# Silu replaced by a tanh form in a fused attention and MLP kernel, and a new place for the output-weight conversions

## The chip, the cores and the metric

The kernel runs on one core of one Trainium2 chip. The metric is the device time of one execution in microseconds, and smaller is better. Before the change three runs took 964.84 to 966.88 us, with a median of 966.83 us.

## The reference

What is computed, cut to what matters here (batch 4, 8 heads, 576 positions, head size 64; 2304 tokens, model width 512, inner width 1536; all in float32):

```python
x = attention(q, k, v)             # heads 0-3: a local window of 32; heads 4-7: strided by 32
xn = x / rms(x) * rms_g
g = xn @ w_gate                    # 512 -> 1536
silu = g * (1.0 / (1.0 + np.exp(-g)))
y = (silu * (xn @ w_val)) @ w_out  # 1536 -> 512
out = ((y @ w_a) * (y @ w_b)) @ w_out2
```

## The kernel before

Matrix products are made in pairs of float32r words: each operand is split into a high part and a low part, and three products (high by high, high by low, low by high; lines 481 to 483) make one. The weights arrive from memory in 64-bit words. A conversion (`conversion`, `words`, `parts`) turns one third of a chunk's weights (gate, value or output) into these two parts: ScalarE runs a Prelu (L137) and a Copy into `cz` (L142), VectorE joins two words (L145), ScalarE casts the high part (L150), and GpSimd or VectorE subtracts it (L151). `cz` has two buffers for the gate and value weights and one for the output weights, so the conversions of the output weights run one behind the other.

The first half of the kernel handles the tokens in six blocks t = 0 to 5 of 384. Each block runs over 12 chunks fc of the inner width. For a chunk, TensorE makes `g_ps` and `v_ps` (12 matmuls each, in three PSUM banks with the tag `gv`). VectorE multiplies `g_ps` by the reciprocal norm `ri[t]` into `sg` (L774), ScalarE applies Silu in place (L776), and VectorE multiplies by `v_ps` into `h` (L787; in block 0 `h` is `v_ps` itself). `split` casts `h` to its high part on ScalarE (L506) and makes the low part on VectorE (block 0) or GpSimd (L507). One chunk later TensorE uses the two parts for the output products `y`. The temporaries `sg` and `h` share five buffers of the tag `t`.

Block 0 also converts the first layer's weights while it uses them: `convert1(fc + 1)` for gate and value, and the conversion of the output weights of chunk fc, which is stored to memory and reloaded in the later blocks. Beside the chunks of block t, the attention of block t+1 runs in steps: the local heads by TensorE with an Exp on ScalarE (L333, L336), the strided heads by GpSimd products (L248, L281) and VectorE reductions (L251, L284), an Exp (L264), then the norm with a Sqrt (L448). Block 5 has no next attention; it starts to convert the second layer's weights instead. The second half (from about 541 us) runs the second layer and has no Silu.

The order of instructions on each engine is fixed when the program is built, by a scheduler that works through the traced instructions with a modelled time. `behind(...)` and `gate(...)` bind it: they put every instruction of their block that runs on the engine of the named instruction behind that one. Two such bindings matter here. `exps` puts the local Exps of block 1's attention behind the newest Silu, and the next Silu behind them (`silu_gate`). The conversion of the output weights of chunks 2 to 11 stands behind the very first Silu, `silu[:1]`, on ScalarE's queue.

Of the kernel before, what the change touches and what calls it, by code (L numbers as in the profile page):

```python
# [14 lines left out]
AF = mybir.ActivationFunctionType  # L15
ALU = mybir.AluOpType
# [7 lines left out]
NTB = B * PB  # L24
# [53 lines left out]
def fused_kernel(ctx: ExitStack, tc: tile.TileContext, qtl, ktl, vl, qs, ks, vs, cst, w1, w2, out):  # L78
# [5 lines left out]
    nc = tc.nc  # L84
# [100 lines left out]
    ri = {}  # L185
# [304 lines left out]
    def tmp(name):  # L490
        return act.tile([128, NTB], F32, tag="t", name=name, bufs=NTMP)

    made = []
    silu, silu_gate = [], []

    @contextmanager
    def behind(instructions):

        with ExitStack() as e:
            for i in instructions:  # L500
                e.enter_context(tc.issue_after(i))
            yield
# [37 lines left out]
    def load_late(which):  # L540
        raw.update(zip(which, load_pair(w1, which, pool)))
# [39 lines left out]
    @contextmanager  # L581
    def gate(fc):

        with behind(silu[:1] if fc > 4 else []), ExitStack() as e:
            for key in GATES[min(fc, len(GATES) - 1)].split():
                e.enter_context(tc.issue_after(s0["st"][key].ins))
            yield
# [25 lines left out]
    def load_wo(t, fc):  # L613
        wt = wo[t, fc] = wo_tile()
        nc.sync.dma_start(wt.rearrange("p a n -> p (a n)").bitcast(F32), wod[fc])
# [14 lines left out]
        for n in part:  # L630
            steps[n]()

    def exps(steps):

        def together(f, key):
            def g():
                with behind([silu[-1]]):
                    f()
                silu_gate.append(steps["st"][key].ins)
            return g  # L640

        for n in ("lexp0", "lexp1", "lexp2"):
            steps[n] = together(steps[n], "exp")


    forms = {}

    def form_tile(k, spare=False):
# [93 lines left out]
    for t in range(NB):  # L742
        if t == 1:
            apool.close()
            pool = apool.enter_context(tc.tile_pool(name="attn", bufs=1))
        if t == NB - 1:
            apool.close()
            cpool.close()
            pool = p2.enter_context(tc.tile_pool(name="forms", bufs=1, reuse_waits="tile"))
            early = [f for k in (4, 5, 0, 1, 2, 3) for f in convert_forms(k, k < 4)]  # L750
        nxt = attention(t + 1, pool, psum, itertools.cycle(["att"])) if t + 1 < NB else None
        if t == 0:
            exps(nxt)
        x = [xt[t, cc] for cc in range(NCC)]
        for fc in range(NFC):
            if t > 0 and fc == 0:
                load_wo(t, 0)
            g_ps = psum.tile([128, 512], F32, tag="gv", name="g_ps", bufs=3)
            mm_in(g_ps[:, :NTB], gv[fc], 0, x)
            v_ps = psum.tile([128, 512], F32, tag="gv", name="v_ps", bufs=3)  # L760
            mm_in(v_ps[:, :NTB], gv[fc], 1, x)
            if t == 0 and fc + 1 < NFC:
                with gate(fc + 1):
                    convert1(fc + 1)
                if fc + 2 == NFC:
                    load_late([(NFC - 2, 2), (NFC - 1, 2)])
            if t == NB - 1:
                slab[fc] = wgt.tile([128, 4 * DM], F32 if fc in (0, 1, 11) else F32R, tag="gv", name="slab", bufs=NFC)
                with behind(made):
                    run(early[len(early) * fc // NFC:len(early) * (fc + 1) // NFC])  # L770
                    for k in [k for k in x0 if k <= fc]:
                        run(x0.pop(k))
            sg = tmp("sg")
            nc.vector.tensor_tensor(sg, g_ps[:, :NTB], ri[t], op=ALU.mult)  # L774
            with behind(silu_gate):
                silu.append(nc.scalar.activation(sg, sg, AF.Silu).ins)  # L776
            silu_gate[:] = []
            if fc == 1 and t > 0:
                evac_y(t - 1)
            if nxt is not None:  # L780
                attention_slot(nxt, fc)
            if prev is not None:
                emit_y(*prev)
            if t > 0 and fc + 1 < NFC:
                load_wo(t, fc + 1)
            h = tmp("h") if t else v_ps[:, :NTB]
            made[:] = [nc.vector.tensor_tensor(h, sg, v_ps[:, :NTB], op=ALU.mult).ins]  # L787
            hl[t, fc] = split(h, engine(HLO0[fc] if t == 0 else HLO[t]))
            if t == 0:
                wt = wo[0, fc] = wo_tile()  # L790
                with gate(fc + 1), behind(silu[:1] if fc > 1 else []):
                    run(conversion(raw.pop((fc, 2)), wt, pool, engine(WLO[fc][2]), LOW[fc][2], True))
                nc.sync.dma_start(wod[fc], wt.rearrange("p a n -> p (a n)").bitcast(F32))
                if fc % 2 and units:
                    load_units(1)
            prev = (t, fc)
# [140 lines left out]
    steps = [(ps, g, p) for ps in (range(0, 3), range(3, 6)) for g in range(NB // 2) for p in ps]  # L937
# [99 lines left out]
```

## Time and profile before

| | before |
|---|---|
| median of 3 runs | 966.83 us (964.84 to 966.88) |
| the profiled execution: its time / its span | 967.4 us / 965.6 us |
| TensorE matmuls busy | 937.1 us, 97% |
| VectorE busy | 621.5 us, 64% |
| ScalarE busy | 425.3 us, 44% |
| GpSimd busy | 539.5 us, 56% |
| mean granted TensorE clock | 0.985 |

The span runs from the first to the last instruction of the program; the time also holds what lies around it (1.8 us here). A busy TensorE works through pipelined matmuls; its idle time and the stretches at a lower granted clock are what another order of work can give back.

### The profile page before, as it was taken

To read this page: it belongs to the slowest core of one execution; us is meant where nothing else is said; L and a number is where in the kernel's file an instruction comes from. 1 tells how busy PE (TensorE), PEld (TensorE's weight loads), DVE (VectorE), ACT (ScalarE), POOL (GpSimd) and SP (SyncE) were. 2 spreads that over 40 slices of the span, in tenths; PEclk is the share of its full clock that TensorE was granted. 3 is DMA by queue.
4 is the path that set the end of the run, shared out by engine and by line. 5 is a ranking of instruction groups with operands and counts; after the bars stand their busy time and mean duration, and the time that the engine had idled before them with its cause. 6 is when DMAs were issued, how large, how long until landed. Compare 5 with 4: busy or idle time off the path is not lost.

```text
span 965.6 us, 14099 instructions
## 1 busy us (share of the span) xinstructions
PE 937.1 (97%) x5318; PEld 888.2 (92%) x5318; DVE 621.5 (64%) x900; ACT 425.3 (44%) x795; POOL 539.5 (56%) x407
## 2 busy tenths in 40 slices
PE   5998999999999999999999899999999999999998
PEld 4898999999999999999999898899999998999996
DVE  5658858658819895986666378658655655564534
ACT  5988646344433434434555455436425422122110
POOL 3567946558649677878479545655724423123211
PEclk6899999999999999999999999999999999999999
DMA  9974286537535563532788884996993974754701
GB/s 342 408 262 151 89 288 218 151 96 225 165 104 161 161 204 102 185 105 87 284 324 306 329 306 166 402 415 247 385 373 114 345 274 165 284 205 168 267 2 66
DMA packets 57363, 215.55 MB, mean 223 GB/s; under 512 B 5968, under 2 KB 14544, under 8 KB 51664
## 3 DMA queue, kind: packets, MB, share of 16 engines
q1 hardware_dynamic: 57296, 214.66, 61.3%
q8 instruction: 42, 0.69, 0.3%
q14 instruction: 25, 0.20, 0.1%
HBM read 172.17 MB, written 42.47 MB: 222 GB/s over the span
## 4 chain that ended last, share of the span: by engine, by line
PE 65%; DMA 11%; DVE 7%; POOL 7%; ACT 4%; issue 4%; SPq 0%; DVEq 0%; ACTq 0%; POOLq 0%
PE o L916 5%; PE o L918 5%; PE o L917 5%; DMA raw<-in_w 4%; POOL prod L248 4%; PE Y L862 4%; PE Y L861 4%; PE Y L860 4%; DMA gv_raw<-in_w 3%; PE y L482 3%; PE y L481 3%; PE g_ps L483 3%; PE y L483 3%; PE g_ps L482 3%; PE g_ps L481 3%
## 5 line engine op out<-in xcount | busy, mean ns | idle before, releaser
L151 POOL TENSOR_TENSOR hl<-c,hl 128x384 fp32r<-128x384 f32 x72 | 77.9, 1082 | 181.0 <-ACT hl L150 174.4
L248 POOL TENSOR_TENSOR prod<-kv_t,qs_t 128x512 f32<-128x512 f32 (+12 forms) x57 | 108.3, 1921 | 15.3 <-DMA kv_t<-in_ks 8.2
L481 PE MATMUL v_ps<-xx,gv 128*128 128x384 f32 x288 | 97.7, 339 | 1.9 <-DVE sg L774 1.8
L482 PE MATMUL y<-hl,wo 128*128 128x384 f32 x288 | 98.1, 341 | 1.1 <-POOL hl L507 1.1
L281 POOL TENSOR_TENSOR prod<-kv_t,S_t 128x512 f32<-128x512 f32 (+12 forms) x57 | 86.2, 1526 | 21.1 <-issue 7.1
L482 PE MATMUL v_ps<-xx,gv 128*128 128x384 f32 x288 | 97.9, 340 | 0.0
L483 PE MATMUL v_ps<-xx,gv 128*128 128x384 f32 x288 | 97.8, 340 | 0.0
L481 PE MATMUL g_ps<-xx,gv 128*128 128x384 f32 x288 | 97.5, 339 | 0.0
L483 PE MATMUL g_ps<-xx,gv 128*128 128x384 f32 x288 | 97.3, 338 | 0.0
L482 PE MATMUL g_ps<-xx,gv 128*128 128x384 f32 x288 | 96.9, 337 | 0.0
L867 DVE TENSOR_TENSOR c<-c,Y 128x384 f32<-128x384 f32 x108 | 59.0, 551 | 58.8 <-PE Y L862 53.5
L507 POOL TENSOR_TENSOR hl<-h,hl 128x384 fp32r<-128x384 f32 x60 | 64.1, 1069 | 58.4 <-ACT hl L506 57.3
L483 PE MATMUL y<-hl,wo 128*128 128x384 f32 x288 | 95.0, 338 | 0.0
L284 DVE TENSOR_REDUCE xs_t<-prod 128x64 f32<-128x448 f32 (+17 forms) x57 | 85.7, 1521 | 9.7 <-POOL prod L281 9.5
L481 PE MATMUL y<-hl,wo 128*128 128x384 f32 x288 | 85.0, 343 | 7.0 <-ACT hl L506 5.4
L916 PE MATMUL o<-slab,hl 128*128 128x512 f32 x216 | 84.7, 393 | 1.8 <-DVE slab L925 1.3
L917 PE MATMUL o<-slab,hl 128*128 128x512 f32 x216 | 84.5, 392 | 0.0
L918 PE MATMUL o<-slab,hl 128*128 128x512 f32 x216 | 83.2, 394 | 0.0
L150 ACT CAST hl<-c 128x384 fp32r<-128x384 f32 x72 | 37.0, 514 | 93.8 <-DVE c L897 93.5
L776 ACT ACTIVATE sg<-sg 128x384 f32<-128x384 f32 x72 | 38.0, 528 | 86.4 <-DVE sg L774 86.0
L862 PE MATMUL Y<-slab,form 128*128 128x384 f32 x216 | 73.0, 338 | 0.0
L861 PE MATMUL Y<-slab,form 128*128 128x384 f32 x216 | 73.0, 338 | 0.0
(137 smaller groups left out, 2491.4 us busy)
## 6 DMA issues: line engine op xcount, KB each, us to landing
form<-formd SPq DMA_DIRECT2D x32, 1792.0 KB, 10.7
wo<-wod SPq DMA_DIRECT2D x60, 512.0 KB, 3.8
raw<-in_w SPq DMA_DIRECT2D x40, 512.0 KB, 7.3
gv_raw<-in_w SPq DMA_DIRECT2D x32, 512.0 KB, 10.2
formd<-form SPq DMA_DIRECT2D x6, 1792.0 KB, 7.5
formd<-forms SPq DMA_DIRECT2D x6, 1792.0 KB, 12.8
slab<-x2d SPq DMA_DIRECT2D x24, 384.0 KB, 4.0
wod<-wo SPq DMA_DIRECT2D x12, 512.0 KB, 3.4
```

Of the source, the lines that this page charges most:

```text
L151: lo_eng.tensor_tensor(lo, x, hi.bitcast(F32), op=ALU.subtract)
L248: nc.gpsimd.tensor_tensor(pr, st["ks", g][:, :, :n, :], st["qs"][:, heads(g), mm:mm + 1, :].to_broadcast([128, G, n, D]), op=ALU.mult)
L281: st["pvm"] = nc.gpsimd.tensor_tensor(pr, st["vs", g][:, :, :n, :], st["S"][:, heads(g), mm, :n, None].to_broadcast([128, G, n, D]), op=AL ...
L284: st["pvr"] = nc.vector.tensor_reduce(st["xs"][:, mm, heads(g), :], pr.rearrange("p g n d -> p g d n"), axis=X, op=ALU.add)
L481: nc.tensor.matmul(out_ps, w_hi, x_hi, start=start, stop=False)
L482: nc.tensor.matmul(out_ps, w_hi, x_lo, start=False, stop=False)
L483: nc.tensor.matmul(out_ps, w_lo, x_hi, start=False, stop=stop)
L861: nc.tensor.matmul(bank(n), hi, x[p][:, 1, c], start=False, stop=False, skip_group_check=not begins)
L862: nc.tensor.matmul(bank(n), lo, x[p][:, 0, c], start=False, stop=c == 1, skip_group_check=not begins)
L916: nc.tensor.matmul(o, h[:, 0, cols], w[0], start=n == 0, stop=False)
L917: nc.tensor.matmul(o, h[:, 0, cols], w[1], start=False, stop=False)
L918: nc.tensor.matmul(o, h[:, 1, cols], w[0], start=False, stop=n == len(chunks) - 1)
```

## The change

Silu(x) is computed as x/2 (1 + tanh(x/2)). VectorE's first multiplication of a chunk takes a factor 0.5 along and becomes a scalar-tensor-tensor. ScalarE applies Tanh into a new temporary `th` of the tag `t`. VectorE multiplies x/2 into `v_ps` in place, and a further scalar-tensor-tensor makes (th + 1) times that into `h`. The binding of the Exps in block 0 (`exps`, `silu_gate`) goes away. The conversion of the output weights of chunk n (from 2 on) stands behind the tanh of chunk n-2 and no longer behind the first Silu alone.

```diff
-    silu, silu_gate = [], []
+    silu = []
...
-    def exps(steps):
-        def together(f, key):
-            def g():
-                with behind([silu[-1]]):
-                    f()
-                silu_gate.append(steps["st"][key].ins)
-            return g
-        for n in ("lexp0", "lexp1", "lexp2"):
-            steps[n] = together(steps[n], "exp")
...
-        if t == 0:
-            exps(nxt)
...
             sg = tmp("sg")
-            nc.vector.tensor_tensor(sg, g_ps[:, :NTB], ri[t], op=ALU.mult)
-            with behind(silu_gate):
-                silu.append(nc.scalar.activation(sg, sg, AF.Silu).ins)
-            silu_gate[:] = []
+            nc.vector.scalar_tensor_tensor(sg, g_ps[:, :NTB], 0.5, ri[t], op0=ALU.mult, op1=ALU.mult)
+            th = tmp("th")
+            silu.append(nc.scalar.activation(th, sg, AF.Tanh).ins)
...
-            h = tmp("h") if t else v_ps[:, :NTB]
-            made[:] = [nc.vector.tensor_tensor(h, sg, v_ps[:, :NTB], op=ALU.mult).ins]
+            v = v_ps[:, :NTB]
+            nc.vector.tensor_tensor(v, sg, v, op=ALU.mult)
+            h = tmp("h") if t else v
+            made[:] = [nc.vector.scalar_tensor_tensor(h, th, 1.0, v, op0=ALU.add, op1=ALU.mult).ins]
...
-                with gate(fc + 1), behind(silu[:1] if fc > 1 else []):
+                with gate(fc + 1), behind(silu[max(fc - 2, 0):max(fc - 1, 1)] if fc > 1 else []):
                     run(conversion(raw.pop((fc, 2)), wt, pool, engine(WLO[fc][2]), LOW[fc][2], True))
```

## Rows read from the trace of the kernel before

**Rows 1.** Stretches by stage: length, busy time (instructions) per engine, granted clock, DMA share, GB/s.

```profile
43.00:133.00 90.00, 83.11 (x492) 79.37 (x491) 66.34 (x90) 72.83 (x135) 61.33 (x36) 0.96 0.52 189
...
297.00:380.00 83.00, 83.00 (x518) 80.94 (x516) 66.92 (x83) 31.99 (x53) 62.15 (x40) 1.00 0.51 163
380.00:463.00 83.00, 82.77 (x511) 80.25 (x511) 68.22 (x81) 35.46 (x58) 67.12 (x42) 1.00 0.41 134
```

**Rows 2.** Waits of PE over the span: total us, times, longest us.

```profile
PE y L481 <- ACT hl L506: 5.4, 3, 2.1
...
PE v_ps L481 <- DVE sg L774: 1.8, 3, 1.0
```

**Rows 3.** Timeline of PE: start, length, instruction, idle time before it and its releaser.

```profile
51.78 0.97 PE L481 MATMUL y<-hl,wo 128*128 128x384 f32 x4 [1.85 <-ACT hl L506]
...
89.75 0.96 PE L481 MATMUL y<-hl,wo 128*128 128x384 f32 x4 [2.13 <-ACT hl L506]
...
124.72 0.63 PE L481 MATMUL g_ps<-xx,gv 128*128 128x384 f32 x1
...
132.83 0.96 PE L481 MATMUL y<-hl,wo 128*128 128x384 f32 x4 [1.39 <-ACT hl L506]
```

**Rows 4.** Stretches of 10 us, columns as in rows 1.

```profile
50.00:60.00 10.00, 8.22 (x38) 8.22 (x39) 5.45 (x8) 10.00 (x17) 3.62 (x2) 0.83 1.04 407
...
90.00:100.00 10.00, 9.84 (x58) 8.95 (x59) 7.57 (x17) 9.01 (x15) 4.26 (x3) 0.83 0.43 159
100.00:110.00 10.00, 10.00 (x74) 9.52 (x69) 9.74 (x8) 7.39 (x12) 10.00 (x7) 1.00 0.14 54
110.00:120.00 10.00, 10.00 (x61) 9.77 (x60) 9.36 (x12) 5.54 (x12) 9.45 (x7) 1.00 0.31 107
```

**Rows 5.** Timeline of ACT in block 0, the first stretch.

```profile
48.87 0.55 ACT L776 ACTIVATE sg<-sg 128x384 f32<-128x384 f32 x1
...
51.23 0.50 ACT L506 CAST hl<-v_ps 128x384 fp32r<-128x384 f32 x1
...
59.58 2.03 ACT L150 CAST gv<-cz 128x1024 fp32r<-128x1024 f32 x2
```

**Rows 6.** Groups by form on ACT from 43 to 60: busy us, mean ns, idle before.

```profile
L137 ACT ACTIVATE gv_raw<-gv_raw 128x512 f32<-128x512 f32 x6 | 3.9, 698 | 0.0
...
L137 ACT ACTIVATE raw<-raw 128x512 f32<-128x512 f32 x2 | 1.5, 726 | 0.0
```

**Rows 7.** Timeline of POOL in block 0.

```profile
60.74 4.76 POOL L151 TENSOR_TENSOR gv<-cz,gv 128x1024 fp32r<-128x1024 f32 x2 [6.68 <-DMA gv_raw<-in_w]
...
123.22 1.13 POOL L399 TENSOR_TENSOR xx<-x_t,xx 128x384 fp32r<-128x384 f32 x1 [1.19 <-ACT xx L398]
```

**Rows 8.** Timeline of DVE in block 0: the multiplication by the norm of chunk 5.

```profile
76.63 0.55 DVE L774 TENSOR_TENSOR sg<-g_ps,rinv 128x384 f32<-128x384 f32 x1
```

**Rows 9.** Timeline of ACT in block 0, the second stretch.

```profile
84.58 1.28 ACT L776 ACT_TABLE_LOAD   x1
85.87 0.53 ACT L776 ACTIVATE sg<-sg 128x384 f32<-128x384 f32 x1
...
92.57 1.28 ACT L264 ACT_TABLE_LOAD   x1
```

**Rows 10.** Groups on ACT over the span: the table loads in front of Silu.

```profile
L776 ACT ACT_TABLE_LOAD x20 | 25.7, 1283 | 33.5 <-DVE sg L774 25.7 <-DVE lrs L347 6.3 <-DVE ssm L271 1.3
```

**Rows 11.** Groups on DVE over the span.

```profile
L774 DVE TENSOR_TENSOR sg<-g_ps,rinv 128x384 f32<-128x384 f32 x72 | 39.3, 547 | 42.3 <-PE g_ps L483 42.2
...
L787 DVE TENSOR_TENSOR h<-sg,v_ps 128x384 f32<-128x384 f32 x60 | 32.7, 545 | 34.6 <-PE v_ps L483 18.4 <-ACT sg L776 16.1
...
L787 DVE TENSOR_TENSOR v_ps<-sg,v_ps 128x384 f32<-128x384 f32 x12 | 6.7, 555 | 5.8 <-ACT sg L776 3.4 <-PE v_ps L483 2.3
```

**Rows 12.** Instructions of line 314 on DVE: ns min/median/max, first and last start, forms.

```profile
L314 DVE SCALAR_TENSOR_TENSOR s_t<-att,cst_sb x18: 545/558/676, 8.8 to 405.2; 128x384 f32<-128x384 f32 x12, 64x512 f32<-64x512 f32 x6
```

## The prediction

> **What bounds the kernel now.** I read the stages first. From 133 us on TensorE (PE) has no gap to speak of: blocks 2 to 4 show it busy for 83.0 of 83 us while VectorE (DVE) is busy for 67 to 68 [rows 1]. There, faster or slower helpers change nothing until one of them makes PE wait. Block 0, from 43 to 133 us, is different: PE is busy for 83.1 of 90 us at a granted clock of 0.96, and ScalarE (ACT) works for 72.8 us, DVE for 66.3 and GpSimd (POOL) for 61.3 [rows 1]. A change to Silu can pay there, because Silu stands in ACT's queue.
>
> The waits of PE say where. The largest that has to do with Silu is the output product waiting for the cast of the hidden chunk: 5.4 us in 3 waits [rows 2]. The timeline gives the places: 1.85 us before 51.78, 2.13 us before 89.75, 1.39 us before 132.83 [rows 3]. After the first two the granted clock of a 10 us stretch is 0.83 [rows 4]; between the levels 2.4 and 1.2 GHz that is 3.4 us at the lower one, which costs 1.7 us of work each time. PE had idled just before. So the three waits are worth at most 5.4 + 2 x 1.7 = 8.8 us.
>
> Now each wait's cause. *First:* Silu of chunk 1 runs at 48.87 and the cast of hidden chunk 0 at 51.23 [rows 5], on an ACT that is never idle here. Ahead of them stand Prelus of output weights needed much later: from 43 to 60 us there are eight 128x512 Prelus, 698 to 726 ns each, counted singly [rows 6]. One is for chunk 2; the other seven, by the order of their tiles, are for chunks 3 to 9. The same crowd delays the casts of the gate and value weights at 59.58 [rows 5], and POOL, which makes the low parts, has idled 6.68 us when it begins at 60.74 [rows 7]. *Second:* chunk 5's `sg` is ready at 77.2 [rows 8], but its Silu runs at 85.87 behind a table load [rows 9]: the binding put it behind the Exps. *Third:* chunk 11 comes at the end of the attention and of the weight conversions, with the Sqrt and its table change in the way.
>
> **The change part by part.**
>
> *The later output-weight conversions.* Chunk n's Prelu now follows the tanh of chunk n-2. Up to the cast at 59.58 the Prelus of chunks 5 to 9 fall away, as their tanhs (3 to 7) come later: 5 instructions. Issued back to back they overlap: the eight fill 3.9 + 1.5 us of busy time [rows 6], 0.67 us each, and their starts lie closer still. I take 0.56 us, the low end, since the neighbours overlap too: 2.8 us (high end 3.5). Of these, three Prelus, 1.7 us, fall away ahead of the cast at 51.23, about the first wait. The work moves to after 62 us; if ACT has no hole there, it costs the same 2.8 us later. Does the new binding itself hold anything up? What queues behind the Prelu is its chunk's Copy, which needs the one `cz` buffer in any case, and that is released by POOL's low part of the chunk before. Tanh n-2 is two chunks ahead of the use, so I cost this at nothing. No DMA is added; the stores and weight loads that follow a conversion on SP's queue keep their order. If a tanh were late by a chunk, those loads would be late too.
>
> *The Exps unbound.* Chunk 5's tanh can follow its `sg` at 77.2 instead of waiting for 85.87. The 2.13 us wait then goes, but PE can only use it as far as weights are ready; the conversions, not Silu, are late next. So I don't add this wait to the 2.8 us: both are the same lead, and POOL's start sets it.
>
> *Table loads.* 20 loads stand before Silu at 1283 ns [rows 10]. At most six of them follow a Sqrt, one for each block; 14 come from Exp, and each pairs with a load back. If Tanh runs under the table that Exp has loaded, 28 loads go, 35.9 us of ACT. After block 0 ACT is busy for 32 to 35 of 83 us [rows 1] and PE's waits are not on it: worth nothing. In block 0 the loads at 84.58 and 92.57 [rows 9] stand in a full ACT; the first belongs to the chunk already counted, but it also delays the weight casts behind it. I take two loads, 2.6 us, for the lead of the conversions at 100 us. Bounds: nothing, if other engines hold the conversions, and 8.8 - 2.8 = 6.0 us, what is left of the waits. No row shows a Tanh, so the other possibility (no load goes) is a rival.
>
> The Trainium skill, "ScalarE: Activation LUTs", section "Table sets: the hidden batching unit", lists tanh with exp in one set, so that the two need one load. No run here shows it yet; by it, the 28 loads go.
>
> *DVE.* The first multiplication becomes a scalar-tensor-tensor from PSUM: 558 ns [rows 12] for 547 [rows 11]. The multiplication into `v_ps` costs 555, as block 0's does now [rows 11]. The last one is again 558 where `h` took 545. Added: 11 + 555 + 13 = 0.58 us for each chunk, 41.7 us over 72 chunks. Each added instruction reads one operand from PSUM, as those two groups do, and they stay near 550 ns while POOL works. In block 0 there is no room between 100 and 120 us: DVE is busy for 9.74 + 9.36 of 20 us [rows 4], with conversions and reductions that the next block's attention needs. Four chunks (8 to 11) pass DVE from there to the end: 4 x 0.58 = 2.3 us lost. Bounds: 0, if chunks fall in holes, and 12 x 0.58 = 7.0 us if all of block 0 counts.
>
> *Blocks 1 to 5.* 12 x 0.58 = 7.0 us for each block on a DVE with 15 to 16 free of 83 in blocks 3 and 4 [rows 1]. It fits as a sum, not at every place: PE already waits for `sg` to free its bank, 1.8 us in 3 waits [rows 2], and a late `sg` comes one instruction later. The last two steps add 0.57 us between `v_ps` and the cast, with a chunk of PE work as cover; without it, each chunk pays 0.57. I take one such slip, 0.5 us. Bounds: 0 and 3.5 us (six slips of 0.58). The third temporary needs its five buffers sooner: `th` of chunk n+2 reuses `h` of chunk n, which the output products of chunk n have used by then. Nothing.
>
> *Sum.* -2.8 - 2.6 + 2.3 + 0.5 = -2.6 us. From the profiled execution's 967.4 that gives 964.8. That execution lies 0.6 us above the median of the runs (966.83), so I expect a median of **964.2 us**.
>
> **The rivals.** A difference under 0.2%, 1.9 us, is about what can't be told from none.
>
> *The lead is swallowed (about 966.8).* TensorE gains its 2 to 3 us before 90 us, then waits for block 1's inputs: the last low part of `xx` runs from 123.22 on POOL until 124.35 [rows 7], and the first product that needs it starts at 124.72 [rows 3]. There is no slack, so what does not speed up the attention is lost. For it: that row. Against: the output product of chunk 11 ends the block at 132.83, not this one.
>
> *DVE becomes the bound (slower).* Place: 100 to 124 us. The attention's reductions and the joins of the last weights share DVE with the added steps. If ACT's lead doesn't reach that chain, it ends 2.3 us later, PE waits at 124.7, and the median is 966.8 + 2.3 = 969.1. It decides as soon as the lead at 100 us is under 2.3 us. For it: DVE's 19.1 of 20 us. Against: ACT's holes there (7.39 and 5.54 of 10 us) show that part of DVE's queue waits for others [rows 4].
>
> *Tanh has a table of its own.* Then the loads stay, and unbound Exps mix with the tanhs of block 0: four groups of Exps, each now possibly with a load on both sides, up to four loads more than now, 5.1 us on a full ACT. With -2.8 + 2.3 + 0.5 + 5.1 that is 971.9.
>
> *All waits close.* 8.8 us less, 966.8 - 8.8 = 958.0, if DVE finds room.
>
> **How the numbers follow.** Forecast (961 to 965.5) 0.45; swallowed 0.20; DVE bound 0.23; a table of its own 0.06; all waits close 0.06. The bound of 0.2% lies at 964.9 and 968.8. Faster: most of the forecast and the last case, 0.47. Same: the rest of the forecast and the swallowed case, 0.25. Slower: 0.28, the two others, as 969.1 lies just beyond. The range leaves out most of the last case and of the own table: 959.0 to 970.0. Faster and slower share it; the likeliest case's own range is 961 to 965.5.
>
> **What would show it.** Right: table loads down by about 28; the casts near 59.6 and POOL's start near 60.7 come 2 to 3 us earlier; chunk 5's tanh within 2 us of its `sg`; no wait of PE near 90 us; DVE's busy time up by some 42 us to about 663; block 0 ends about 3 us earlier and the later blocks keep their lengths. Wrong: a wait of PE for the cast or for `sg` at new places in blocks 2 to 4; an added step that takes more than 0.6 us; another order of instructions in the later blocks, which the scheduler makes anew; or a first product of block 1 that starts where it does now.

## The result, and the profile after

The changed kernel takes 971.02 us (median of 7 runs, 968.49 to 971.74) where the kernel before took 965.21 us beside it on the same chip (7 runs, 964.61 to 966.88). The ratio is 1.0051, 95% interval 1.0038 to 1.0064: slower by 0.5%, 4.9 us between the means (the medians lie 5.8 us apart), where 2.6 us less were forecast. The profiled execution took 971.74 us with a span of 970.0 us.

The page's busy time of each engine, over the span:

```profile
PE 937.3 (97%) x5318; PEld 886.0 (91%) x5318; DVE 663.8 (68%) x972; ACT 388.4 (40%) x767; POOL 541.0 (56%) x407
```

DVE has 42.3 us more (663.8 - 621.5), ACT 36.9 us less, PE the same. So PE's work did not grow: the added time is PE's idle time. The groups of the added and changed steps on DVE, and of the table loads on ACT (busy us, mean ns):

```profile
L759 DVE SCALAR_TENSOR_TENSOR sg<-g_ps,rinv 128x384 f32<-128x384 f32 x72 | 39.5, 548 | 32.1 <-PE g_ps L483 32.1
L771 DVE TENSOR_TENSOR v_ps<-sg,v_ps 128x384 f32<-128x384 f32 x72 | 39.9, 554 | 30.3 <-PE v_ps L483 29.3
L773 DVE SCALAR_TENSOR_TENSOR h<-th,v_ps 128x384 f32<-128x384 f32 x60 | 32.9, 549 | 7.1 <-ACT th L761 4.4
...
L761 ACT ACT_TABLE_LOAD x6 | 7.7, 1283 | 0.1
L448 ACT ACT_TABLE_LOAD x5 | 6.4, 1283 | 0.1
```

Every step has the price that [rows 11, 12] gave it, so the durations are not what failed. With one load at each of two more lines, 13 table loads are left of 41; the 28 that went are those that the prediction counted [rows 10].

The stages, columns as in [rows 1]:

```profile
43.00:133.00 90.00, 82.34 (x493) 77.71 (x492) 75.17 (x103) 67.31 (x130) 60.41 (x36) 0.98 0.51 187
...
297.00:380.00 83.00, 81.50 (x504) 78.51 (x503) 71.33 (x92) 24.11 (x47) 60.38 (x38) 1.00 0.50 158
380.00:463.00 83.00, 81.35 (x500) 78.07 (x499) 75.35 (x91) 23.37 (x46) 66.61 (x42) 1.00 0.40 129
```

In blocks 3 and 4, where PE had next to no gap, it now works 1.5 and 1.4 us less than in [rows 1]. Block 0 is hardly shorter. Its beginning is: on ACT the first cast of the weights comes 3.9 us earlier [rows 5], where 2 to 3 were predicted, and the tanh of chunk 5 stands right behind its `sg`, at 75.80 and not at 85.87 [rows 9].

```profile
49.40 0.47 ACT L506 CAST hl<-v_ps 128x384 fp32r<-128x384 f32 x1
...
55.64 1.08 ACT L150 CAST gv<-cz 128x1024 fp32r<-128x1024 f32 x1
...
75.80 0.53 ACT L761 ACTIVATE th<-sg 128x384 f32<-128x384 f32 x1
```

PE's timeline shows where the lead goes (the bracket is the idle time before, with its releaser). The wait of 1.85 us at 51.78 [rows 3] has shrunk to 0.30, and the granted clock from 50 to 60 us is 1.00 where it was 0.83 [rows 4]. By chunk 2 the output product starts 5.5 us earlier than before (58.4 for 63.9). Then three new waits stand between 81 and 90 us:

```profile
49.92 0.79 PE L481 MATMUL y<-hl,wo 128*128 128x384 f32 x3 [0.30 <-ACT hl L506]
...
83.31 0.41 PE L481 MATMUL g_ps<-xx,gv 128*128 128x384 f32 x1 [2.02 <-DVE sg L759]
...
87.36 0.62 PE L358 MATMUL att<-cst_sb,s_t 128*96 128x128 f32 x4 [1.73 <-ACT pt L368]
...
89.82 0.69 PE L481 MATMUL v_ps<-xx,gv 128*128 128x384 f32 x1 [1.15 <-DVE sg L759]
...
334.65 0.44 PE L482 MATMUL y<-hl,wo 128*128 128x384 f32 x1 [0.63 <-POOL hl L507]
...
349.85 0.45 PE L482 MATMUL y<-hl,wo 128*128 128x384 f32 x1 [0.76 <-POOL hl L507]
...
413.65 0.44 PE L481 MATMUL g_ps<-xx,gv 128*128 128x384 f32 x1 [1.41 <-DVE h L773]
```

Two of the three wait for `sg`, a DVE step. The stretches of 10 us, first of the kernel before and then of the changed one:

```profile
70.00:80.00 10.00, 10.00 (x69) 9.68 (x69) 9.66 (x16) 7.98 (x18) 9.38 (x7) 1.00 0.70 237
80.00:90.00 10.00, 7.16 (x43) 6.56 (x42) 7.46 (x10) 9.65 (x26) 9.14 (x5) 1.00 0.28 93
```

```profile
70.00:80.00 10.00, 9.74 (x67) 9.05 (x66) 10.00 (x12) 5.98 (x14) 8.12 (x5) 1.00 0.27 92
80.00:90.00 10.00, 5.11 (x29) 4.21 (x28) 9.83 (x17) 9.54 (x27) 6.44 (x4) 0.98 0.42 127
90.00:100.00 10.00, 10.00 (x51) 9.68 (x52) 8.49 (x16) 6.97 (x13) 5.51 (x5) 0.85 0.31 122
```

DVE has 19.83 of 20 us from 70 to 90 (17.12 before), PE falls to 5.11 of 10 us, and its clock to 0.85 right after: the second dip of [rows 4] is not gone. But not all of these 19.83 us are work. DVE's timeline, and then POOL's:

```profile
77.50 2.88 DVE L145 SCALAR_TENSOR_TENSOR cz<-gv_raw,cz 128x512 uint32<-128x512 uint32 x1
...
82.62 0.54 DVE L759 SCALAR_TENSOR_TENSOR sg<-g_ps,rinv 128x384 f32<-128x384 f32 x1
...
84.12 3.41 DVE L145 SCALAR_TENSOR_TENSOR cz<-gv_raw,cz 128x1024 uint32<-128x1024 uint32 x1
...
89.22 0.54 DVE L759 SCALAR_TENSOR_TENSOR sg<-g_ps,rinv 128x384 f32<-128x384 f32 x1
```

```profile
76.92 2.92 POOL L151 TENSOR_TENSOR gv<-cz,gv 128x1024 fp32r<-128x1024 f32 x1
...
84.08 2.36 POOL L151 TENSOR_TENSOR gv<-cz,gv 128x1024 fp32r<-128x1024 f32 x1
```

The two joins take 2.88 and 3.41 us, where the shortest of their forms in block 0 take 0.67 and 1.22. Each began during a GpSimd instruction and ended only 0.5 and 1.1 us after it (the section on the hardware comes back to this). Both late `sg` stand behind such a join, which is 2.2 us longer each time than it need be; the added product in between takes 0.53 to 0.55 us. The third wait, at 87.36, is for ACT, busy for 9.54 of these 10 us.

In blocks 3 and 4 the waits are those for POOL's low part and for `h`. DVE's timeline ahead of two of them, 349.85 and 413.65, shows a long reduction of the attention (`S_t<-prod`, `xs_t<-prod`) between the two steps behind `v_ps`:

```profile
344.84 0.56 DVE L771 TENSOR_TENSOR v_ps<-sg,v_ps 128x384 f32<-128x384 f32 x1
345.31 1.65 DVE L284 TENSOR_REDUCE xs_t<-prod 128x64 f32<-128x832 f32 x1
346.88 0.55 DVE L773 SCALAR_TENSOR_TENSOR h<-th,v_ps 128x384 f32<-128x384 f32 x1
...
411.41 0.55 DVE L771 TENSOR_TENSOR v_ps<-sg,v_ps 128x384 f32<-128x384 f32 x1
411.87 1.27 DVE L251 TENSOR_REDUCE S_t<-prod 128x17 f32<-128x1088 f32 x1
413.07 0.53 DVE L773 SCALAR_TENSOR_TENSOR h<-th,v_ps 128x384 f32<-128x384 f32 x1
```

So `h` begins 1.7 to 2.0 us after the step ahead of it, where it could have begun 0.5 us after. In the second case PE's `g_ps` product waits 1.41 us, to 413.65, for the bank that this `h` reads and then frees. The wait at 334.65 is another: its two steps stand close together (330.18 and 330.84), and the low part is late behind POOL's own products of the attention.

```profile
330.40 3.24 POOL L281 TENSOR_TENSOR prod<-kv_t,S_t 128x832 f32<-128x832 f32 x2 [0.81 <-POOL s_t L348]
```

### The profile page after: what moved, and what is told of

Its sections match the earlier page's. It is cut to its first block, busy times and chain, and to the rows that moved or that the text cites. A ratio compares the mean times of both kernels' runs of the same rounds, so it can differ in the third digit from the quotient of the medians.

```text
span 970.0 us, 14244 instructions
## 1 busy us (share of the span) xinstructions
PE 937.3 (97%) x5318; PEld 886.0 (91%) x5318; DVE 663.8 (68%) x972; ACT 388.4 (40%) x767; POOL 541.0 (56%) x407
## 4 chain that ended last, share of the span: by engine, by line
PE 65%; DVE 15%; DMA 8%; issue 5%; POOL 4%; ACT 3%; SPq 0%; DVEq 0%; POOLq 0%; ACTq 0%
PE o L902 5%; PE o L904 5%; PE o L903 5%; PE Y L848 4%; PE Y L847 4%; PE Y L846 4%; DMA gv_raw<-in_w 3%; PE y L482 3%; PE y L483 3%; PE y L481 3%; PE g_ps L483 3%; PE g_ps L481 3%; PE g_ps L482 3%; PE v_ps L482 3%; PE v_ps L481 3%
## 5 line engine op out<-in xcount | busy, mean ns | idle before, releaser
L248 POOL TENSOR_TENSOR prod<-kv_t,qs_t 128x512 f32<-128x512 f32 (+12 forms) x57 | 104.5, 1853 | 22.9 <-DVE S_t L251 10.1
L482 PE MATMUL y<-hl,wo 128*128 128x384 f32 x288 | 97.7, 341 | 2.8 <-POOL hl L507 2.3
L483 PE MATMUL y<-hl,wo 128*128 128x384 f32 x288 | 93.7, 336 | 0.0
L481 PE MATMUL y<-hl,wo 128*128 128x384 f32 x288 | 82.2, 346 | 2.5 <-DMA wo<-wod 1.9
L761 ACT ACTIVATE th<-sg 128x384 f32<-128x384 f32 x72 | 37.8, 525 | 91.9 <-DVE sg L759 84.3
L506 ACT CAST hl<-h 128x384 fp32r<-128x384 f32 x60 | 30.8, 513 | 109.3 <-DVE h L773 105.2
L150 ACT CAST hl<-c 128x384 fp32r<-128x384 f32 x72 | 36.9, 513 | 93.7 <-DVE c L883 93.5
L848 PE MATMUL Y<-slab,form 128*128 128x384 f32 x216 | 73.1, 339 | 0.0
```

The source lines that it names most:

```text
L248: nc.gpsimd.tensor_tensor(pr, st["ks", g][:, :, :n, :], st["qs"][:, heads(g), mm:mm + 1, :].to_broadcast([128, G, n, D]), op=ALU.mult)
L481: nc.tensor.matmul(out_ps, w_hi, x_hi, start=start, stop=False)
L482: nc.tensor.matmul(out_ps, w_hi, x_lo, start=False, stop=False)
L483: nc.tensor.matmul(out_ps, w_lo, x_hi, start=False, stop=stop)
L848: nc.tensor.matmul(bank(n), lo, x[p][:, 0, c], start=False, stop=c == 1, skip_group_check=not begins)
```

## The experiments

The theory after the result: each added step is cheap by itself, but it stands on the chain from `g_ps` to the words of `h`, on an engine that works in order; PE waits wherever that chain lies behind other DVE work. Three rivals: DVE has too much work in all, wherever the step stands; the new place of the output-weight conversions does the harm; the unbound Exps do.

All runs, with the ratio to the kernel before, and with PE's level at the end of blocks 0, 2 and 5 against the kernel before (us, from one profiled execution each; positive is late). The level is the start of the last output product of the block. But PE does not always have the same work ahead of that product. In the change nine `g_ps` matmuls of the next block run just before it, which in the kernel before run behind it, from 133.63 us on:

```profile
132.13 0.33 PE L481 MATMUL g_ps<-xx,gv 128*128 128x384 f32 x1
...
133.69 0.33 PE L481 MATMUL y<-hl,wo 128*128 128x384 f32 x1
```

So 0.18 us, the mean distance of two such matmuls, is taken off for each matmul of the next block that an execution had begun by then and the kernel before had not (9 for the change at the end of block 0, 11 at the end of block 2, none at the end of block 5; in e7 31 at the end of block 0). In e17 and e18 eight of them are smaller ones of the attention, at 0.10 us.

```
                                             median   ratio   95% interval      b0    b2    b5
the change                                   971.02  1.0051  1.0038..1.0064   -0.7  -1.8   4.2
e1  Silu, conversions moved                  973.05  1.0081  1.0066..1.0096    0.2   4.6   4.8
e2  tanh, conversions as before              971.96  1.0065  1.0052..1.0078   -0.2  -1.3   5.4
e3  the change without the product           958.62  0.9927  0.9915..0.9938   -6.3  -6.8  -7.9
e4  before plus one product on the chain     978.28  1.0129  1.0113..1.0145    2.1   3.5  11.5
e5  the change, tanh in block 0 alone        969.27  1.0040  1.0028..1.0052   -0.6   3.2   3.2
e6  before, tanh in blocks 1 to 5            970.36  1.0056  1.0044..1.0068   -1.3  -2.2   3.7
e7  as e5, product of block 0 on GpSimd      972.90  1.0078  1.0066..1.0090    0.6   5.8   5.7
e9  before, Exps unbound                     968.61  1.0044  1.0031..1.0056    1.2   2.1   2.2
e10 before plus one product beside the chain 972.12  1.0064  1.0052..1.0077    4.1   3.1   4.6
e11 before, tanh in blocks 1 and 2           964.30  0.9983  0.9974..0.9992   -1.6  -2.5  -2.7
e12 the change, tanh in blocks 0 to 2        964.88  0.9986  0.9977..0.9994   -2.3  -3.3  -3.1
e13 the change, no product in block 0        967.58  1.0016  1.0007..1.0025   -4.6  -5.6   0.7
e14 the change, factor first                 986.07  1.0200  1.0186..1.0214    2.9   4.0  18.7
e15 factor first in blocks 1 to 5            981.72  1.0160  1.0146..1.0174   -1.7  -0.7  13.4
e16 as e3, conversions as before             964.19  0.9979  0.9971..0.9988   -2.0  -2.1  -3.2
e17 as e14, x/2 kept in PSUM                 973.74  1.0080  1.0061..1.0099   -2.1  -0.9   7.4
e18 as e15, x/2 kept in PSUM                 973.62  1.0078  1.0058..1.0099   -2.0  -2.6   6.5
e19 the change, reductions behind h          972.01  1.0072  1.0053..1.0090    0.4  -0.6   5.8
```

One caution for this table: e6, e11, e15 and e18 leave block 0's code as it was, and each engine runs its instructions there in the same order as in the kernel before up to 124 us; yet block 0 ends 1.3 to 2.0 us earlier. That is the spread of single executions: the profiled one of the kernel before took 967.4 us, 2.2 more than the median of 965.21. So a level of under some 2 us in one profile says nothing by itself.

**What the product costs.** e3 leaves the line of x/2 out; e4 adds a product of the same shape to the kernel before, on the same chain; neither computes the reference's values.

```diff
-            nc.vector.tensor_tensor(v, sg, v, op=ALU.mult)                    # e3
...
+            v = v_ps[:, :NTB]                                                 # e4, ahead of h
+            nc.vector.tensor_tensor(v, ri[t], v, op=ALU.mult)
```

> The changed kernel without the product of x/2 and the value half (the hidden value is then (1 + tanh) times the value half, so this leaves part of the computation out). VectorE has the same number of instructions per chunk as before; table loads, bindings and conversions are those of the changed kernel. Theory A: the loss of blocks 3 to 5 goes and block 0 keeps part of its lead of 3 to 5 us; 959 to 964. Theory B: 969 to 972 as with the change.

> The kernel before, Silu and all bindings kept, with one more VectorE instruction per chunk: the value half is multiplied in place by the norm once more (so the output is not the reference's), 555 ns as the added product of the change. Theory A: slower by 4 us or more, 969 to 974, with waits of TensorE for sg and for the hidden parts in blocks 3 to 5. Theory B: the added instruction is hidden, 965 to 967.

Both go theory A's way and beyond its ranges. The same product is worth 12.4 us under the tanh (971.02 - 958.62) and 12.6 us under the Silu (978.28 against 965.71 of the kernel before beside it). It takes 39.9 us of DVE; a third of that reaches the end. From the table, of the 12.1 us between the change and e3 at the end of block 5 (4.2 + 7.9), 5.0 have come by the end of block 2 and 7.1 in blocks 3 to 5; in blocks 1 and 2 neither has a gap of PE to speak of. Without it, the gains are at least as large as predicted, and PE's stretch from 80 to 90 us of e3 is full, although DVE is busy for 9.10 us there, and for all of the 10 us before:

```profile
80.00:90.00 10.00, 10.00 (x60) 9.65 (x58) 9.10 (x18) 10.00 (x30) 4.71 (x4) 1.00 0.48 151
```

e13 leaves the product out in block 0 alone (the same line under `if t > 0`):

> The changed kernel with the product of x/2 and the value half left out in block 0 alone (part of the computation of block 0 is missing); blocks 1 to 5 are those of the change. If the 12.4 us that the product costs in all split into 7 us in block 0 and 5 us in blocks 3 to 5: 963 to 966. If block 0 costs little: 968 to 971.

The time falls by 3.4 us (971.02 to 967.58), to a value between the two expectations. Block 0 ends 4.6 us early, and block 2 5.6, but at the end of block 5 the kernel is 0.7 us late: blocks 3 to 5 lose 6.3 us, as much as in the change (6.0). So there are two places of loss, and the later one does not come from the earlier. Block 0's is 3.4 to 5.0 us, by the medians and by the levels against e3; the other is the larger.

Whether in block 0 the product itself does the harm, or the joins, stays open: the 19 joins up to the end of block 0 (from 40 us) take 29.4 us in the change, 24.5 in e3 and 25.4 in the kernel before, and no run holds them fixed.

**The chain or the load.** e10 gives the kernel before the same product, but behind `h` and into a spare tile that nobody reads.

```diff
+            spare = tmp("spare")
+            nc.vector.tensor_tensor(spare, ri[t], v_ps[:, :NTB], op=ALU.mult)
```

> The kernel before with one more VectorE instruction per chunk that nobody waits for: value half times norm into a spare buffer, after h. It is the same work as the added product, but beside the chain from the value half to the cast. If the 12 us of the added product are VectorE's time (queue full): slower by 8 us or more. If they are the longer chain from v_ps to the cast: 965 to 968.

It takes 544 ns, 72 times. The median, 6.1 us over the kernel before beside it, is that of neither expectation; the blocks say more. PE is busy for 83.0 and 82.1 of 83 us in blocks 3 and 4, though DVE is nearly as busy there as in the changed kernel (143.0 against 146.7 of 166 us):

```profile
297.00:380.00 83.00, 83.00 (x520) 81.20 (x518) 68.54 (x97) 31.91 (x53) 63.95 (x41) 1.00 0.52 164
380.00:463.00 83.00, 82.09 (x508) 79.51 (x507) 74.47 (x92) 33.60 (x53) 69.16 (x41) 1.00 0.38 119
```

In blocks 3 to 5 e10 loses 1.5 us (3.1 to 4.6) where e4, with the same product on the chain, loses 8.0 (3.5 to 11.5). It is thus mostly the place on the chain that costs there, not DVE's load. In block 0 e10 loses 4.1 us, about what the product on the chain costs. That does not yet make it the load: in block 0 DVE also makes the low part of `h`, the spare product stands ahead of it, and in 6 of the 12 chunks directly ahead of an `sg`; PE waits 5.9 us for `sg` in this block. So in block 0 the product is not beside the chain, and load and chain are not told apart. The joins are not the cause there, as they take only 22.9 us in e10.

**The two other parts alone.** e1 moves only the conversions under the Silu, e9 only unbinds the Exps, e2 is the change with the conversions at their old place, e16 is e3 with that place.

```diff
-                with gate(fc + 1), behind(silu[:1] if fc > 1 else []):        # before, e2, e9, e16
+                with gate(fc + 1), behind(silu[max(fc - 2, 0):max(fc - 1, 1)] if fc > 1 else []):  # e1
...
-        if t == 0:                                                            # e9
-            exps(nxt)
```

> The kernel before with one edit: the output weights of chunk n stand behind the Silu of chunk n-2. Silu, the binding of the Exps and VectorE's work stay. Theory A (the time is lost to the 0.58 us that each chunk adds on VectorE): without that work the lead that the later Prelus give ScalarE up to 60 us can survive, 0 to 3 us faster than before (962 to 965.5). Theory B (the time is lost to the new place of the conversions or the order that follows from it): most of the 5 us shows here, 968 to 971.

> The kernel before with the binding of the Exps in block 0 taken away and nothing else: Silu and its table loads stay, old place of the conversions. If the lead of block 0 came from the binding that fell away: 960 to 963. If it came from the table loads that fell away: 965 to 970, with more loads than 41.

> The changed kernel with the output weights behind the first tanh alone, as before. Theory A: the added VectorE work is all there, so blocks 3 to 5 lose as in the changed kernel; 969 to 972. Theory B: near the kernel before, 964 to 967.

> The changed kernel without the product of x/2 and the value half (part of the computation is missing, as in the run at 958.6) and with the output weights back behind the first tanh. If the new place of the conversions carries the lead of block 0: 962 to 966. If the lead comes from the table loads and the unbound Exps: 957 to 960.

Each part alone makes the kernel slower, e1 even by more than its theory B. e1 gains 5.3 us at the output product of chunk 2 and gives it back from 82 us on, so that it is level at the end of block 0 (0.2); another 4.4 us go in block 1 (0.2 to 4.6 by its end), where PE waits 2.5 us for `s_t` from DVE and 0.8 for POOL's low part. PE's timeline of e1:

```profile
88.29 1.06 PE L358 MATMUL att<-cst_sb,s_t 128*96 128x128 f32 x4 [3.80 <-ACT pt L368]
...
113.20 0.44 PE L481 MATMUL y<-hl,wo 128*128 128x384 f32 x1 [1.69 <-ACT wo L150]
```

The conversions that no longer stand ahead of 60 us stand at 80 to 115 us now, ahead of the attention's `pt` (with two table loads) and of their own use. e9 likewise waits for `wo` from ACT, 1.2 to 1.7 us at 83, 108 and 118 us, and keeps 43 table loads. The move pays 5.6 us where the table loads are gone and DVE has no product to make (e3 against e16); with the product in place (the change against e2) the two intervals overlap. The move's worth is not a term of its own.

**Where the tanh can stand.** The tanh form in some blocks only (a test on `t` around it):

> Tanh form, unbound Exps and the new place of the conversions in block 0 alone; blocks 1 to 5 have Silu and VectorE's two instructions as before. Theory A (VectorE's added instruction costs time in block 0 and again in blocks 3 to 5): block 0 comes out level, as in the changed kernel's trace, and blocks 1 to 5 lose nothing; 963.5 to 966.5. Rival (the loss is made by the order in which block 0 hands over, and the later blocks only show it): 969 to 972.

> The reverse: block 0 is that of the kernel before (Silu, bound Exps, old place of the conversions), blocks 1 to 5 have the tanh form. Theory A: slower by the 4 to 6 us that the changed kernel loses from block 2 on; 969 to 972. Rival: 964 to 967.

> Tanh form in blocks 1 and 2 alone, all else as before (block 0 with Silu and its bindings, blocks 3 to 5 with Silu). If the cost of the added product lies where VectorE is full, these two blocks cost nothing, since in the changed kernel's trace they gain 0.9 us: 962.5 to 965.5. If every block pays, 967 to 969.

> The change in blocks 0 to 2, Silu in blocks 3 to 5. The changed kernel's trace is 1.7 us ahead of the one before at the end of block 2 and loses 5.9 us after it; with VectorE's work of blocks 3 to 5 as before that lead should stay: 963 to 966. If the loss is one of order that block 3 makes anew: 967 to 971.

Blocks 3 to 5 lose 5.9 us with it in e6 (-2.2 to 3.7) and nothing to speak of without it in e11 and e12 (-0.2 and +0.2); blocks 1 and 2 lose nothing with it in any of these runs. e11 and e12 are faster than both kernels, by 0.14% to 0.17%; their intervals end just below 1, and the difference is under the 0.2% that the prediction set for telling a change from none. Most of e11's level, 1.6 of 2.5 us at the end of block 2, is there by the end of block 0, which its edit does not touch. e5 came out as its rival had it: it loses 3.8 us in block 1 (-0.6 to 3.2), where its Silus begin. PE waits there for the cast of `hl` and the norm of `s_t`, 1.9 us at 169 to 171 us, and its granted clock over the block is 0.98. Which part of the new order makes them late was not tested.

e7 makes the product of block 0 on GpSimd:

```diff
+                h = tmp("h")
+                nc.vector.scalar_tensor_tensor(h, th, 1.0, v, op0=ALU.add, op1=ALU.mult)
+                made[:] = [nc.gpsimd.tensor_tensor(h, sg, h, op=ALU.mult).ins]
```

> Like the run with tanh in block 0 alone, but the added multiplication stands on GpSimd: VectorE makes (1 + tanh) times the value half, GpSimd multiplies by x/2. VectorE's work in block 0 is then that of the kernel before, and all of the result is computed. Theory A: block 0 keeps most of the 6.6 us that it gained without the product, less what GpSimd's 12 x 1.0 us takes back; 959 to 963. Rival (any added work in block 0, on whichever engine, eats the lead): 964 to 968.

The time, 972.9, is above both expectations. At the end of block 0 e7 is about level (0.6), at the end of block 1 5.8 us late, against 3.2 in e5. `h` now lies in SBUF and not in `v_ps`, and DVE's low part of it takes 2.53 us in the place that PE's longest wait goes back to (it took 0.55 us from `v_ps`, at 58.55 in e14). DVE's timeline, and then POOL's:

```profile
108.04 2.53 DVE L507 TENSOR_TENSOR hl<-h,hl 128x384 fp32r<-128x384 f32 x1
110.49 1.74 DVE L145 SCALAR_TENSOR_TENSOR cz<-raw,cz 128x512 uint32<-128x512 uint32 x1
112.16 0.54 DVE L777 SCALAR_TENSOR_TENSOR h<-th,v_ps 128x384 f32<-128x384 f32 x1
```

```profile
107.77 2.38 POOL L151 TENSOR_TENSOR gv<-cz,gv 128x1024 fp32r<-128x1024 f32 x1
```

DVE ends 0.4 us after POOL does (110.57 and 110.15), and the join behind it is stretched in the same way. The next `h`, whose tanh was done at 108.9, has to wait behind it until 112.16, and PE waits 3.46 us for the bank that it frees. So e7 tells little of the place of the product: it changed another step's operands.

**One step behind `v_ps`.** If the two steps behind `v_ps` are the harm, then one of them can be made earlier: the factor first, and a single product when `v_ps` comes.

```diff
             silu.append(nc.scalar.activation(th, sg, AF.Tanh).ins)
+            nc.vector.scalar_tensor_tensor(th, th, 1.0, sg, op0=ALU.add, op1=ALU.mult)
...
-            nc.vector.tensor_tensor(v, sg, v, op=ALU.mult)
-            made[:] = [nc.vector.scalar_tensor_tensor(h, th, 1.0, v, op0=ALU.add, op1=ALU.mult).ins]
+            made[:] = [nc.vector.tensor_tensor(h, th, v, op=ALU.mult).ins]
```

> The changed kernel with its two last VectorE steps regrouped: (1 + tanh) times x/2 is made as soon as the tanh is there, and one multiplication follows the value half. VectorE has the same three steps per chunk, all of the result is computed. Theory C (blocks 3 to 5 lose to two steps behind v_ps with a reduction between them, block 0 to VectorE's time): blocks 1 to 5 lose under 1 us, block 0 stays level; 964 to 967. Theory A (VectorE's time everywhere): 970 to 973, more if the new step, with two operands in SBUF, is slower than 550 ns.

> The same regrouping in blocks 1 to 5 alone, block 0 as before the change. Its partner, the tanh form with two steps behind v_ps in the same blocks, took 970.4. Theory C: the 5 us go, 962 to 966. Theory A: 969 to 972.

Both are far slower, beyond the ranges of both theories; e14's expectation names the reason, a slower step with two SBUF operands, and the groups of e14 show a step that is not like the others:

```profile
L762 DVE SCALAR_TENSOR_TENSOR th<-th,sg 128x384 f32<-128x384 f32 x72 | 69.6, 966 | 26.8 <-ACT th L761 25.0
...
L773 DVE TENSOR_TENSOR h<-th,v_ps 128x384 f32<-128x384 f32 x60 | 32.7, 546 | 5.7 <-PE v_ps L483 3.4
```

The step with two SBUF operands takes 966 ns in the mean; 24 of the 72 stand beside no GpSimd instruction and take 495 to 559 ns, the others up to 2439 ns. One of them, DVE's timeline and then POOL's:

```profile
318.38 2.33 DVE L762 SCALAR_TENSOR_TENSOR th<-th,sg 128x384 f32<-128x384 f32 x1
```

```profile
318.00 2.31 POOL L248 TENSOR_TENSOR prod<-kv_t,qs_t 128x832 f32<-128x832 f32 x1
```

POOL ends at 320.3, DVE 0.4 us later. Of the 41 steps that began during a GpSimd instruction 38 end 0.41 or 0.42 us after it: they worked only when POOL had done. e17 and e18 keep x/2 in the PSUM bank of `g_ps`, so that this step has one PSUM operand:

```diff
+            sg = g_ps[:, :NTB]
             nc.vector.scalar_tensor_tensor(sg, g_ps[:, :NTB], 0.5, ri[t], op0=ALU.mult, op1=ALU.mult)
```

> The kernel with the factor first (th = (1 + th) x sg right behind the tanh, then one product with v_ps), with one edit: x/2 is written back into the PSUM bank of g_ps and not into an SBUF tile, so the factor's step reads one operand from PSUM. In e14 that step took 495 to 559 ns where GpSimd was idle and up to 2439 ns beside it, 966 ns in the mean. Theory A (the two SBUF operands beside GpSimd cost e14 its time, and the two steps in a row behind v_ps cost the changed kernel its time): the step takes 550 ns everywhere, DVE's busy time falls by 30 us to about 654, and with a single step behind v_ps blocks 3 to 5 keep their lengths: 963 to 968. Theory B (the factor's step stands at the head of DVE's queue waiting for the tanh and holds up what is behind it): most of e14's loss stays, 976 to 984. Theory C (g_ps now holds its bank until the factor is made): new waits of PE for that step before v_ps or g_ps, over 3 us in all, 970 to 976.

> The same edit in blocks 1 to 5 alone; block 0 and the output-weight conversions as in the kernel before. Theory A: blocks 1 and 2 gain their 1 to 2 us as they do in every kernel with the tanh there, blocks 3 to 5 lose nothing: 962.5 to 965. Theory B: at least half of e15's loss stays, 971 to 980, with DVE standing before the factor's step for 20 us or more over the span. Theory C: waits of PE for the bank of g_ps at 0.3 to 1 us each in blocks 3 and 4, 967 to 971.

```profile
L763 DVE SCALAR_TENSOR_TENSOR th<-th,g_ps 128x384 f32<-128x384 f32 x72 | 39.1, 543 | 30.3 <-ACT th L762 30.3
```

The step takes 543 ns everywhere (494 to 555), and 12.3 us of e14's time and 8.1 us of e15's are gone. But theory A of these expectations is wrong in its second half: with a single step behind `v_ps` blocks 3 to 5 of e18 still lose 9.1 us (-2.6 to 6.5). Its time is that of theory B, and DVE's waits name what can hold the chain up in place of the reduction:

```profile
DVE th L778 <- ACT th L777: 25.5, 28, 5.2
```

In 28 chunks DVE stands with this step at the head of its queue until ACT's tanh is there, 0.9 us in the mean, and what is behind it waits too; how much of the 9.1 us this makes was not tested. Theory C holds in small in e18, where PE waits 2.0 us in blocks 3 to 5 for the bank of `g_ps`, and outright in e17, whose time it gives; PE's waits of e17 from 43 to 545 us:

```profile
PE v_ps L481 <- DVE th L763: 7.4, 5, 4.3
```

**The reductions taken from between.** e19 is the change, with the attention's reductions of blocks 3 to 5 collected and issued behind `h`:

```diff
+            with behind(made):
+                flush()          # the reductions of this slot, kept back until here
```

> The changed kernel with one edit: in blocks 3 to 5 the attention's two kinds of long DVE reductions (S_t<-prod and xs_t<-prod) are issued behind the last step of the chunk beside which they stand (h), and not before its second step. In the order of instructions the changed kernel has such a reduction between the two DVE steps behind v_ps in 11 of the 24 chunks of blocks 3 and 4; here it is 0 of 12 in block 3 and 4 of 12 in block 4. Nothing is added or left out, and DVE works as long. Theory A (the second step is late because a reduction of 1 to 2 us stands ahead of it in DVE's queue): the 0.63 and 0.76 us waits of PE for POOL's low part at 335 and 350 us go, block 3 loses less than 0.5 us where the changed kernel loses 2.2, block 4 at most half of its 2.1, and the median is 966.5 to 969. Theory B (a second step costs wherever it stands, 0.55 us a chunk with no cover): blocks 3 and 4 lose 4 us as before, 970 to 972. Theory C (reductions issued later hold up GpSimd's products, which have two buffers, and with them the attention): PE waits for the attention or for xx at the ends of blocks 3 and 4, and the median is over 973.

In block 3 theory A holds: both waits at 335 and 350 us are gone, one is left (363.47), and the block loses 0.9 us (-0.6 to 0.3) instead of 2.3 (-1.8 to 0.5), a little more than the 0.5 expected. As no reduction stood between the steps ahead of the wait at 335, part of this is the new order. In block 4, which loses 3.5 us instead of 2.1, the reductions come late for their own reader, theory C:

```profile
363.47 0.44 PE L497 MATMUL y<-hl,wo 128*128 128x384 f32 x1 [0.64 <-POOL hl L522]
...
419.62 0.79 PE L496 MATMUL y<-hl,wo 128*128 128x384 f32 x3 [1.14 <-ACT hl L521]
...
463.51 0.91 PE L459 MATMUL att<-sq,ones 128*128 128x384 f32 x2 [2.12 <-POOL sq L453]
```

The wait of 2.12 us is for the next block's norm, behind the attention. The median, 972.0, is theory B's; the blocks point to A and C together.

## Why the prediction was wrong

*What was right.* The table loads (28 fewer), the price of each step, DVE's total (663.8 us), the first casts (55.64 for 59.58), the place of chunk 5's tanh. The Trainium skill, "ScalarE: Activation LUTs", section "Table sets: the hidden batching unit", puts tanh and exp in one set; the trace agrees, with 13 loads for 41.

*The gains, -2.8 and -2.6.* Their sum, -5.4, was near: without the product (e3) the kernel gains 0.73% [0.62, 0.85], 7.0 us, inside the 8.8 us of the waits; by the levels 6.3 of its 7.9 us are there by the end of block 0, where the prediction put them. But they are not two terms. Each part alone loses: the move under Silu costs 0.81% (e1), the unbinding 0.44% (e9). The prediction priced the later conversions as "if ACT has no hole there, it costs the same 2.8 us later" and then counted on the hole; the move pays only when the table loads are gone and DVE has no product to make.

*The failed step: "Blocks 1 to 5", +0.5.* It measured 7.1 us, the change against e3, all of it in blocks 3 to 5 and beyond its bound of 3.5. "A chunk of PE work as cover" was assumed, and a slip was priced at one step, 0.58 us. But what an in-order engine puts between two steps costs too: a reduction of 1.3 to 1.7 us stands there in two of the three waits shown. e10 shows that the load is not the main cause in these blocks, e19 that taking the reductions away shortens block 3, e18 that moving the step ahead of `v_ps` does not help and brings a wait at the head of the queue. What stays open is how the 7.1 us divide between reductions, POOL's own queue and the waits for the tanh, and whether an order exists that keeps both the chain and the attention on time; none of the three tried did.

*The mis-sized term: "DVE", +2.3.* In block 0 it measured 3.4 us (e13) to 5.0 us (e3), inside its bounds of 0 and 7.0. The prediction looked for a full DVE at 100 to 120 us, because [rows 4] showed it there, and counted 4 chunks. That stretch stayed nearly as full (9.12 and 9.14 of 10 us), but the waits came at 80 to 90 us, where DVE rose from 7.46 to 9.83. It also read busy time as work: three of the joins between 100 and 120 us of the kernel before take 5.5 us for 2.6 in their shortest form. And e3 has 19.10 of 20 us at 70 to 90 with PE full, so a full DVE alone does not make PE wait; the chain has to stand behind it.

*The rivals.* "DVE becomes the bound" had the right engine and sign, but the wrong place and only block 0; that its 969.1 lies 2 us from the measured time is luck, as blocks 3 to 5 have no part in it. Swallowed: no, e3 keeps its lead to the end. Own table: no. All waits close (958.0) lies near e3's 958.6, in part by luck: in block 0 of e3 PE still waits 3.7 us, while both dips of the clock are gone (1.00 from 43 to 133 us).

The levels at the end of block 5 give -7.9 + 5.0 + 7.1 = +4.2 us. That this meets the change's own level says nothing, since its distance from e3 was only taken apart; the check is e13, which leaves out the first of the two and gains 3.4 us.

## What to carry to other kernels

An added step is not priced by its duration on an engine that has room, but by the chain it joins: ask what the in-order queue will put ahead of it, and who waits behind it. A window of the trace of before tells who is full in that schedule; when the change brings work forward, look for the next place where that work meets a full engine, and ask how much of the busy time is work. Before two executions are compared at a mark, see that the same work lies ahead of it. Two edits that use the same hole are one term, so test each alone.

## What the runs showed of the hardware

A DVE step with two SBUF operands that begins during a GpSimd instruction waits here for its end. In e14 such a step took 495 to 559 ns alone and up to 2439 ns when it began during a GpSimd instruction, and 38 of 41 ended about 0.4 us after it (320.7 against 320.3); the same step with one operand in PSUM (e17) took 494 to 555 ns all along, beside GpSimd or not. The low part of e7 shows the same pair of numbers (2.53 us beside POOL's 2.38). The joins of block 0 (L145, two SBUF operands) have always done so: from 40 us to the block's end each that began during a GpSimd instruction, ten in the kernel before and ten in the changed one, ended 0.54 to 0.55 us (128x512) or 1.08 to 1.09 us (128x1024) after it. The Trainium skill, "SBUF — State Buffer", section "SBUF: two separate sides", says that the two share a pair of ports under an exclusive lock, which a DVE instruction with two SBUF inputs takes against a GpSimd instruction that reads SBUF; the trace agrees. So the choice of the operand's memory was worth 12 us in e14 and 8 us in e15, more than the whole change (5).
